# Attention and FFN on one core: pooled scores as four products that share two banks with the local scores, transposes of 96 and 128 columns, and the band mask built for one block and spread by VectorE

## The chip, the core and the metric

The kernel runs on one core of a Trainium2 chip. A core has TensorE (PE: matrix products; a product consists of a weight load, PEld, and a pass of the other operand), VectorE (DVE), ScalarE (ACT), GpSimd (POOL) and SyncE (SP, which here only issues DMAs). They run their own instruction streams in order and wait for each other by semaphores. Products are written to PSUM banks of 128 partitions by 512 float32 values; everything else works on SBUF tiles.

The metric is the device time of one execution in microseconds. The time before is the median of three runs, 1004.47 us (1001.52 to 1006.77).

## The reference

Two attentions are added and put through a feed-forward network. The sizes are: batch 8, 8 heads, 576 positions, 64 values a head; 4608 tokens of 512 values, 2048 hidden values.

```python
def _attn_ref(q, k, v):
    factor = 4
    ...
    q_d = q.reshape(B, H, Sd, factor, D).mean(axis=3)      # k_d and v_d likewise
    out_d = sm_attn(q_d, k_d, v_d)                          # softmax attention over 144 pooled positions
    out_up = np.repeat(out_d, factor, axis=2)
    mask = np.abs(pos[:, None] - pos[None, :]) < factor     # local: a band of +-3 positions
    scores = np.where(mask, scale * q @ k.T, -1e9)
    ...
    return out_up + out_local

def _moe_ref(x, w_in, w_out):
    h = x @ w_in
    return (h * np.cos(h)) @ w_out
```

The feed-forward weights come as float64.

## The kernel before

**Units.** The attention is cut into 32 units: 8 batches times 4 pairs of heads. In a unit, the 64 values of one head lie on partitions 0 to 63 and those of the other on 64 to 127. A unit has these parts:

- `u_qk`: SyncE loads queries and keys (L570), VectorE or GpSimd sums groups of four positions into `qkd` (L577, or L574 and L576), pooled queries and keys of 144 columns.
- `u_s`, scores and softmax. The local scores are 48 products of 32 x 32 (L643): 12 blocks of 32 columns on each of four partition groups, 384 columns in one bank. The pooled scores are 6 products (L652): three groups of 64 queries (0 to 63, 64 to 127, 80 to 143), each for two heads, with the 64 queries as weights and 144 keys as the moving operand, into a second bank of three groups of 144 columns. Then VectorE takes maxima and subtracts (`mxl`, `sml`, `mxd`), ScalarE the exponentials (L678, L679, L681), VectorE sums and reciprocals (L684, L686, L688), and VectorE or GpSimd scales (L690).
- `u_t`: VectorE transposes the local probabilities `sml` (L705). TensorE transposes the pooled ones, `smd`, in two halves of 72 keys: `t_mm` makes two transposes of 128 columns (L714) and a product with 2 x 16 columns of the identity (L716), and ScalarE or VectorE copies the bank to `ptd` (L561, L562).
- `u_pv`: values. Pooled products L759, local ones L771, and the sum of both by VectorE (L782); then the result is split into two float16 parts, the feed-forward input.

**Early and late units.** Batches 0 and 1 are "early" (`NEARLY` = 2). There the band mask is put into the bank by a product of the identity `ident_b` with the mask (L637) before the local products are added, so VectorE reads masked scores straight from the bank (L666, L667). In batches 2 to 7, "late", VectorE adds the mask while it reads the bank (L670). Early score banks come from four named banks, a pair for one unit and the other pair for the next; late ones from a ring of three.

**Feed-forward.** `gemm1` (L811) makes 12 products of 384 columns for each of 16 hidden chunks and 12 token tiles; ScalarE and VectorE make h cos h of it (L825 to L831, L387); `gemm2` (L850) has 9 products of 512 columns. The float64 weights are loaded as integers (L410) and split by VectorE and ScalarE (`w_split`, L422 to L463).

**The order.** Every piece is an operation in a planner with an estimated duration. The planner lists operations by priority, gives those with alternatives to one of two engines (sums of queries and keys, copies from PSUM, scaling), and the program is emitted in the order of planned starts. So a changed estimate can change the order everywhere. Where TensorE has a planned gap in the first 300 us, products of `ident_b` with itself fill it (L988); the first 16 stand at the start of the program. SyncE's loads of the first two batches and the weights are in a fixed order: queries and keys of batch 0, values of batch 0, pooled values of batch 1 (L597, into a ring of 7 buffers, `wd`), weights of chunks 0 and 1, queries and keys of batch 1, and the rest of the weights. A pooled-value buffer comes free when the addition over its four rows is done (`v_add`, L605 and L606, on GpSimd or VectorE).

**Constants.** GpSimd makes two identities, sets the float32 mask of 128 x 384 to zero and cuts the band into it with eight selections of 32 x 384 (L351, L353), sets four corners (L356, L357) and casts it (`mask_b`, L358).

Of the kernel before, what the change touches and what calls it, by code (L numbers as in the profile page):

```python
# [24 lines left out]
P = 128  # L25
# [18 lines left out]
PAD = 3  # L44
SP_ = S + 8
NBLK = 2 * NSEG
QG = 64
NQG = -(-SD // QG)
# [7 lines left out]
NWD = 7  # L56
EARLY = {0: dict(s="pa.0 pa.1 po.0 po.1", t="pa.2", v="ph.0 ph.1"),
# [256 lines left out]
def attn_ffn_kernel(ctx: ExitStack, tc: tile.TileContext, qT, kT, vdn, vl, w_in, w_out, out):  # L314
# [24 lines left out]
    mask, mask_b = const.tile([P, NBLK, BS], F32, name="mask"), const.tile([P, NBLK, BS], BF16, name="mask_b")  # L339

    def constants():
        make_identity(nc, ident_b)
        make_identity(nc, ident)
        dve.memset(bquart, -0.25)
        dve.memset(bhalf, -0.5 * PI)
        dve.memset(ones, 1.0)
        dve.memset(tiny, TINY)
        pool.memset(mask, 0.0)
        for i in range(4):
            h = mask[i * BS:(i + 1) * BS]  # L350
            pool.affine_select(out=h, in_=h, compare_op=ALU.is_ge, fill=NEG, base=0,  # L351
                               pattern=[[0, NBLK], [1, BS]], channel_multiplier=-1)
            pool.affine_select(out=h, in_=h, compare_op=ALU.is_ge, fill=NEG, base=2 * PAD,  # L353
                               pattern=[[0, NBLK], [-1, BS]], channel_multiplier=1)
        for h in range(2):
            pool.memset(mask[2 * BS * h:2 * BS * h + BS, 0, 0:PAD], NEG)  # L356
            pool.memset(mask[2 * BS * h + BS:2 * BS * h + 2 * BS, NBLK - 1, BQ + PAD:BS], NEG)  # L357
        pool.tensor_copy(mask_b, mask)  # L358
# [19 lines left out]
    loads = {}  # L378

    def dma(nbytes, fn, r=(), w=(), pw=()):  # L380
        o = pl.op("SP", max(0.45, nbytes / 262e3), fn, r=r, w=w, pw=pw, lat=1.8)
        loads.setdefault((pl.name,) + pl.arg, []).append(o)
        return o
# [238 lines left out]
    def u_s(b, pr):  # L622
        pl.name = "u_s"
        u = st[(b, pr)]
        q, k, qkd, qkg = u["q"], u["k"], u["qkd"], u["qkg"]
        early = b < NEARLY
        sml, smd = ub(b, pr, "sml"), ub(b, pr, "smd")
        bl, bp = bank(b, "s"), bank(b, "s")
        loc, poo = pl.buf(None), pl.buf(None)

        def using(bk, o):
            bk.r.append(o)
            bk.acc.append(o)

        def l_mm():
            if early:
                pe.matmul(bl.get()[:, :NBLK * BS], ident_b, mask_b.rearrange("p s n -> p (s n)"), start=True, stop=False)  # L637
            for a in range(NSEG // 2):
                for i in range(4):
# [386 lines left out]
```

## Time and profile before

| | us |
|---|---|
| three runs | 1006.77, 1004.47, 1001.52 |
| the profiled execution | 1000.71 |
| its span, first to last instruction | 998.9 |
| TensorE busy | 956.5 |
| VectorE busy | 649.1 |
| ScalarE busy | 601.2 |
| GpSimd busy | 220.2 |

The mean granted clock of TensorE was 0.981 of full speed. The rest of the 1000.71 us lies around the span. In the profile, a group's busy time counts the overlap of neighbours on one engine once; the mean is that of one instruction from its start to its end, and neighbours on TensorE and VectorE overlap. The page's 40 slices of the span, in tenths busy, and the granted clock:

```profile
PE   7788889989999999999999999999999999999998
DVE  5968979697878856745555764755555764544443
PEclk8979979999999999999999999999999999999999
```

A slice is 25 us. TensorE is below nine tenths in the first six slices and the eighth, and VectorE is fullest in the first eleven or so. The small products of the units are a small share: the pooled scores, transposes and local products together stand behind the two feed-forward groups L811 and L850, which carry 33% of the chain each.

### The profile page before, as it was taken

Reading aid. Unit: us, or ns where it says so; the run is one execution under the profiler, and the core shown is the slowest. Engines: PE = TensorE matmul, PEld = TensorE weight load, DVE = VectorE, ACT = ScalarE, POOL = GpSimd, SP = SyncE. Lnnn points to the kernel's source line nnn. Section 1 sums busy time; section 2 is a strip of 40 time slices with the busy share of each in tenths; the row PEclk is TensorE's granted clock in tenths of the full one; section 3 lists DMA queues with packets and bytes.
Section 4 is the critical chain, followed back from the end, with each engine's and each line's share of the span. In section 5 each row is a group of like instructions: output and inputs, shape, how many; then the busy total and the mean of one; then the engine's idle time right before and its main releaser. Section 6 shows DMA issues by size and latency. Waiting matters only on the chain.

```text
span 998.9 us, 26495 instructions
## 1 busy us (share of the span) xinstructions
PE 956.5 (96%) x11333; PEld 558.1 (56%) x11333; DVE 649.1 (65%) x1272; ACT 601.2 (60%) x1225; POOL 220.2 (22%) x360
## 2 busy tenths in 40 slices
PE   7788889989999999999999999999999999999998
PEld 5566445545556655655555665655555665555554
DVE  5968979697878856745555764755555764544443
ACT  2736667677887655656465764656555764644543
POOL 4544823241443311301011320401010210000000
PEclk8979979999999999999999999999999999999999
DMA  8632896576645631321100530321010000000000
GB/s 243 242 124 86 231 270 166 111 168 186 151 85 109 149 78 41 81 57 42 46 27 25 129 90 9 91 63 41 34 41 25 19 34 1 2 32 1 32 1 32
DMA packets 41854, 84.81 MB, mean 85 GB/s; under 512 B 4040, under 2 KB 14536, under 8 KB 41736
## 3 DMA queue, kind: packets, MB, share of 16 engines
q1 hardware_dynamic: 35256, 69.15, 21.6%
q0 software_dynamic: 6480, 13.96, 9.5%
q8 instruction: 89, 1.46, 0.6%
q14 instruction: 29, 0.24, 0.1%
HBM read 65.01 MB, written 18.09 MB: 83 GB/s over the span
## 4 chain that ended last, share of the span: by engine, by line
PE 81%; DVE 6%; ACT 3%; issue 3%; DMA 3%; POOL 2%; POOLq 0%; ACTq 0%; DVEq 0%
PE bank L850 33%; PE bank L811 33%; PE bank L771 4%; PE bank L643 3%; PE bank L652 3%; PE bank L759 2%; PE bank L988 1%; PE bank L714 1%; DMA out<-ob 1%; DMA wd<-vdn 1%; DVE wv L427 1%; DVE tr L826 1%; DVE wv L429 1%; DMA wd<-w_in 1%; ACT wd L435 1%
## 5 line engine op out<-in xcount | busy, mean ns | idle before, releaser
L850 PE MATMUL bank<-wo,gh 128*128 128x512 f16 x1152 | 343.9, 380 | 8.6 <-ACT ob L867 7.3
L811 PEld LDWEIGHTS <-wi 128*128 128x128 f16 x2304 | 225.5, 99 | 178.6 <-issue 12.8
L850 PE MATMUL bank<-wo,gl 128*128 128x512 f16 x576 | 218.6, 380 | 1.4 <-POOL gl L387 1.1
L825 ACT ACTIVATE tr<-bank,bquart,hs 128x384 int32<-128x384 f32 x192 | 128.3, 669 | 108.5 <-PE bank L811 102.8
L826 DVE SCALAR_TENSOR_TENSOR tr<-bank,hs,tr 128x384 f32<-128x384 f32 x192 | 117.9, 615 | 115.3 <-ACT tr L825 114.9
L850 PEld LDWEIGHTS <-gh 128*128 128x128 f16 x1152 | 109.5, 99 | 117.8 <-issue 15.4
L829 DVE SCALAR_TENSOR_TENSOR tr<-tr,rho,bank 128x384 f32<-128x384 f32 x192 | 116.8, 609 | 83.1 <-ACT tr L828 82.8
L828 ACT ACTIVATE tr<-tr,bhalf 128x384 f32<-128x384 f32 x192 | 117.4, 613 | 79.5 <-DVE tr L826 78.5
L831 ACT ACTIVATE gh<-tr 128x384 f16<-128x384 f32 x181 | 94.4, 521 | 113.5 <-DVE tr L829 113.2
L387 DVE TENSOR_TENSOR gl<-tr,gh 128x384 f16<-128x384 f32 x170 | 95.6, 563 | 67.5 <-ACT gh L831 66.2
L811 PE MATMUL bank<-x0h,wi 128*128 128x384 f16 x384 | 103.6, 332 | 7.4 <-DVE tr L829 5.2
L811 PE MATMUL bank<-x1h,wi 128*128 128x384 f16 x384 | 102.9, 330 | 0.0
L811 PE MATMUL bank<-x2h,wi 128*128 128x384 f16 x384 | 101.5, 326 | 0.7 <-DVE tr L829 0.7
L811 PE MATMUL bank<-x3h,wi 128*128 128x384 f16 x384 | 101.5, 326 | 0.0
L850 PEld LDWEIGHTS <-gl 128*128 128x128 f16 x576 | 56.5, 98 | 70.7 <-POOL gl L387 1.6
L574 POOL TENSOR_TENSOR qkd<-q 128x144 f32<-128x144 f32 x25 | 14.6, 585 | 264.6 <-PE bank L652 260.8
L811 PE MATMUL bank<-x0l,wi 128*128 128x384 f16 x192 | 63.8, 332 | 0.0
L811 PE MATMUL bank<-x1l,wi 128*128 128x384 f16 x192 | 63.4, 330 | 0.0
L811 PE MATMUL bank<-x3l,wi 128*128 128x384 f16 x192 | 62.6, 326 | 0.0
L811 PE MATMUL bank<-x2l,wi 128*128 128x384 f16 x192 | 62.6, 326 | 0.0
L771 PE MATMUL bank<-sml,vl 32*64 32x24 f32 x3072 | 53.0, 214 | 1.2 <-issue 0.7
L771 PEld LDWEIGHTS bank<-sml,vl 32*64 32x64 f32 x3072 | 49.4, 135 | 8.0 <-issue 5.2
(155 smaller groups left out, 1208.7 us busy)
## 6 DMA issues: line engine op xcount, KB each, us to landing
vl<-vl SPq DMA_DIRECT2D x32, 384.0 KB, 3.5
q<-qT SPq DMA_DIRECT2D x32, 292.0 KB, 3.7
k<-kT SPq DMA_DIRECT2D x32, 292.0 KB, 4.0
out<-ob SPq DMA_DIRECT2D x36, 256.0 KB, 2.7
out<-ob POOLq DMA_DIRECT2D x33, 256.0 KB, 5.8
wd<-w_in SPq DMA_DIRECT2D x16, 512.0 KB, 4.5
wd<-w_out SPq DMA_DIRECT2D x16, 512.0 KB, 6.3
wd<-vdn SPq DMA_DIRECT2D x18, 384.0 KB, 4.4
```

Source lines behind the costliest of these rows:

```text
L387: f = lambda e: lambda: e.tensor_tensor(out=out(), in0=in0(), in1=in1(), op=ALU.subtract)
L643: pe.matmul(bl.get()[BS * w:BS * (w + 1), BS * c:BS * (c + 1)], q.get()[hs, o:o + BS], k.get()[hs, o:o + BS], start=not early, stop=not ea ...
L652: pe.matmul(bp.get()[hs, g * SD:(g + 1) * SD], qkg()[hs, 0, o:o + QG], qkg()[hs, 1, :], start=True, stop=True)
L759: pe.matmul(banks[0].get()[64 * h:64 * h + 64, 2 * SD:3 * SD], vdg()[:, kh, 64 * h:64 * h + 64], ptd.get()[:, kh, h, :], start=(kh == 0), ...
L771: pe.matmul(banks[e].get()[64 * h:64 * h + 64, o:o + BQ], vt.get()[r, a, i, :], sml.get()[r, 4 * a + i, :BQ], start=True, stop=True)
L811: pe.matmul(ph.get()[:, :m], w[:, i, kc, :], x[:, kc, :], start=(n == 0), stop=(n == 3 * KC - 1))
L825: pl.op("ACT", _act(m, True, 2), lambda: act.activation(ti(), h(), AF.Identity, bias=bquart, scale=inv()), r=[ph, hs], w=[tr])
L826: pl.op("DVE", _dvs(m), lambda: dve.scalar_tensor_tensor(out=tr.get(), in0=h(), scalar=inv(), in1=ti(), op0=ALU.mult, op1=ALU.subtract), r ...
L828: pl.op("ACT", _act(m, False, 1), lambda: act.activation(tr.get(), tr.get(), AF.Sin, scale=2.0 * PI, bias=bhalf), w=[tr], tab="sin")
L829: pl.op("DVE", _dvs(m), lambda: dve.scalar_tensor_tensor(out=tr.get(), in0=tr.get(), scalar=rho(), in1=h(), op0=ALU.mult, op1=ALU.mult), r ...
L831: pl.op("ACT", _act(m, False), lambda: act.activation(gh.get(), tr.get(), AF.Copy), r=[tr], w=[gh], alts=[("DVE", _dve(m / 2), lambda: dve ...
L850: pe.matmul(o, (gh, gh, gl)[k].get()[:, sl], wo.get()[:, (0, 1, 0)[k]], start=(c == c0 and k == 0), stop=(c == c1 - 1 and k == 2))
```

## The change

Five things change.

- **Pooled scores (`d_mm`).** Four products take the place of six. Two have 128 queries (0 to 127) as weights, one for each head (L661 in the changed file); two have 64 queries (80 to 143), one for each head (L664). `HQ` = 48: the last 48 queries are used from these.
- **Banks.** Local and pooled scores are laid over the same two banks. `lcut`: local blocks 0 to 7 lie in bank 0, columns 0 to 255, and blocks 8 to 11 in bank 1 behind the pooled groups. `gcut`: pooled groups 0 (head 0) and 1 (the narrow products) lie in bank 1, group 2 (head 1) in bank 0 behind the local blocks. VectorE's instructions that read scores are split by bank: 8 and 4 blocks, 2 and 1 groups. The mask product of early units is split into 256 and 128 columns. The exponentials of a unit count as readers of both banks.
- **Transposes (`t_mm`).** Two of 96 columns (one for each head) and one of 128 columns, for each half of the keys.
- **Constants.** The band is cut into 128 x 32 first (eight selections of 32 x 32), then GpSimd makes the identities; VectorE casts the band to all 12 blocks (`mask`, now bfloat16) and sets the corners. Late units add the bfloat16 mask.
- **Planner.** The estimates of the changed operations are new numbers, and SyncE's loads get a dependency on a load further back than `AHEAD` = 2^40 bytes.

```diff
-QG = 64
-NQG = -(-SD // QG)
+QG, HQ = 64, 48
+NQG = 3
...
+AHEAD = 1 << 40
...
+        pool.memset(band, 0.0)
+        for i in range(4):
+            h = band[i * BS:(i + 1) * BS]
+            pool.affine_select(out=h, in_=h, compare_op=ALU.is_ge, fill=NEG, base=0, pattern=[[1, BS]], channel_multiplier=-1)
...
         make_identity(nc, ident_b)
+        dve.tensor_copy(mask, band.unsqueeze(1).broadcast_to([P, NBLK, BS]))
...
-        bl, bp = bank(b, "s"), bank(b, "s")
+        banks = [bank(b, "s"), bank(b, "s")]
...
+        lcut, gcut = ((0, 0, 8), (1, 2 * SD, NBLK)), ((1, 0, 2), (0, 8 * BS, NQG))
...
         def d_mm():
-            for g in range(NQG):
-                for h in range(2):
-                    hs, o = slice(64 * h, 64 * h + 64), min(g * QG, SD - QG)
-                    pe.matmul(bp.get()[hs, g * SD:(g + 1) * SD], qkg()[hs, 0, o:o + QG], qkg()[hs, 1, :],
-                              start=True, stop=True)
+            to = [t() for _, _, _, t in cuts(gcut, SD)]
+            for h in range(2):
+                hs = slice(64 * h, 64 * h + 64)
+                pe.matmul(to[h][:, 0], qkg()[hs, 0, :P], qkg()[hs, 1, :], start=True, stop=True)
+            for h in range(2):
+                hs = slice(64 * h, 64 * h + 64)
+                pe.matmul(to[0][hs, 1], qkg()[hs, 0, SD - QG:], qkg()[hs, 1, :], start=True, stop=True)
...
-            using(bl, pl.op("DVE", _dve(n), lambda: dve.tensor_tensor(out=sml.get(), in0=lq(), in1=mask, op=ALU.add), r=[loc], w=[sml]))
+                using(k, "DVE", _dve(w), lambda c=c, src=src: dve.tensor_tensor(out=sml.get()[:, c], in0=src(), in1=mask[:, c], op=ALU.add),
+                      r=[loc], pw=[sml])
...
+        for k, c, w, src in cuts(gcut, SD):
+            using(k, "DVE", _dve(w), lambda c=c, src=src: dve.tensor_reduce(out=mxd.get()[:, c], in_=src(), axis=AX.X, op=ALU.max, negate=True),
+                  r=[poo], pw=[mxd])
...
-                for g in range(NQG - 1):
-                    pe.transpose(to[:, :, g * QG:(g + 1) * QG], smd.get()[:, g, ks], ident)
-                w = SD - (NQG - 1) * QG
-                pe.matmul(to[:, :, SD - w:], smd.get()[:, NQG - 1, ks], ident.rearrange("p (h n) -> p h n", h=2)[:, :, QG - w:],
-                          start=True, stop=True)
+                for h in range(2):
+                    pe.transpose(to[:, h, :SD - HQ], smd.get()[:SD - HQ, 2 * h, ks], ident[:SD - HQ, :SD - HQ])
+                pe.transpose(to[:, :, SD - QG:], smd.get()[:, 1, ks], ident)
```

**TensorE, late units.** The rows from one unit's transposes to another's scores, in a late batch; feed-forward rows that stand between are left out. A row gives line, operation, result and operands, shape and count. Before:

```order
L714 MATMUL bank<-ident,smd 72x2x64 x2
L716 MATMUL bank<-ident,smd 72x2x16
L643 MATMUL bank<-k,q 32x32 x48
L652 MATMUL bank<-qkd 64x144 x6
L850 LDWEIGHTS gh
```

After:

```order
L733 MATMUL bank<-ident,smd 72x96 x2
L734 MATMUL bank<-ident,smd 72x2x64
L652 MATMUL bank<-k,q 32x32 x48
L661 MATMUL bank<-qkd 128x144 x2
L664 MATMUL bank<-qkd 64x144 x2
```

Six pooled products became two wide and two narrow ones, in the same place behind the local products; the narrow product of the identity (L716) became a whole transpose, and the two transposes before it have fewer columns.

**VectorE, the first unit's scores.** From the sums of the first two units (`qkd`) to the first unit's pooled maximum, and what follows. Before:

```order
L577 TENSOR_REDUCE qkd<-k 128x144
L666 TENSOR_REDUCE mxl<-bank 128x12
L577 TENSOR_REDUCE qkd<-q 128x144
L667 TENSOR_TENSOR sml<-bank,mxl 128x384
L673 TENSOR_REDUCE mxd<-bank 128x3
```

After:

```order
L577 TENSOR_REDUCE qkd<-k 128x144
L677 TENSOR_REDUCE mxl<-bank 128x8
L677 TENSOR_REDUCE mxl<-bank 128x4
L679 TENSOR_TENSOR sml<-bank,mxl 128x256
L679 TENSOR_TENSOR sml<-bank,mxl 128x128
L688 TENSOR_REDUCE mxd<-bank 128x2
L688 TENSOR_REDUCE mxd<-bank 128x1
L577 TENSOR_REDUCE qkd<-k 128x144
L577 TENSOR_REDUCE qkd<-q 128x144
```

Three instructions became six, and the sum of the next unit's queries moved behind them. Behind unit 1's pooled maximum (L688) there now stands the addition of pooled values `wd` (L605, L606), which was 19 rows further on. In the changed program the first maximum waits for the wide and narrow pooled products as well, since they write the same banks, and the mask product of units 2 and 3 waits for the exponentials of units 0 and 1.

**GpSimd, the start.** From the sums of queries and keys to the scaling of the first local probabilities (L690 before, L709 after). Before:

```order
L574 TENSOR_TENSOR qkd<-k 128x144
L576 TENSOR_TENSOR qkd<-qkd,k 128x144 x2
L690 TENSOR_TENSOR sml<-sml,su 128x384
L605 TENSOR_TENSOR wd<-wd 72x512
L606 TENSOR_TENSOR vd<-wd 72x256
```

After:

```order
L576 TENSOR_TENSOR qkd<-qkd,k 128x144 x2
L605 TENSOR_TENSOR wd<-wd 72x512
L606 TENSOR_TENSOR vd<-wd 72x256
L605 TENSOR_TENSOR wd<-wd 72x512
L606 TENSOR_TENSOR vd<-wd 72x256
L605 TENSOR_TENSOR wd<-wd 72x512
L606 TENSOR_TENSOR vd<-wd 72x256
L709 TENSOR_TENSOR sml<-sml,su 128x384
```

Three additions of pooled values moved ahead of the scaling.

More of the change, by code (lines that the diff above doesn't have):

```diff
@@ L635, in l_mm, with using, cuts @@
+        def using(k, *a, **kw):
+            o = pl.op(*a, **kw)
+            banks[k].r.append(o)
+            banks[k].acc.append(o)
+        def cuts(cut, size):
+            c = 0
+            for k, at, end in cut:
+                yield k, slice(c, end), (end - c) * size, lambda k=k, at=at, n=end - c: banks[k].get()[:, at:at + n * size].rearrange(
+                    "p (c n) -> p c n", n=size)
+                c = end
         def l_mm():
-            if early:
-                pe.matmul(bl.get()[:, :NBLK * BS], ident_b, mask_b.rearrange("p s n -> p (s n)"), start=True, stop=False)
@@ L638, in l_mm @@
[L638 to L639 removed]
+            for k, c, n, to in cuts(lcut, BS):
+                if early:
+                    pe.matmul(to(), ident_b, mask[:, c], start=True, stop=False)
+                for j in range(c.start, c.stop):
                     for e in range(2):
                         for h in range(2):
[L642 to L644 removed]
+                            hs, o, w = slice(64 * h, 64 * h + 64), (8 * (j // 4) + 4 * e + j % 4) * BQ, 2 * h + e
+                            pe.matmul(to()[BS * w:BS * (w + 1), j - c.start], q.get()[hs, o:o + BS], k_.get()[hs, o:o + BS],
+                                      start=not early, stop=not early or j == c.stop - 1)
@@ L679, in exps @@
             act.activation(sml.get(), sml.get(), AF.Exp, scale=0.125)
-            for g in range(NQG):
-                act.activation(smd.get()[:, g], dq()[:, g], AF.Exp, bias=mxd.get()[:, g:g + 1], scale=1.0 / 128.0,
-                               accum_out=sud()[:, g:g + 1])
-        using(bp, pl.op("ACT", _act(n, False) + 1.2, exps, r=[poo], w=[mxd, sml, smd], pw=[su, part], tab="exp"))
+            for _, c, _, src in cuts(gcut, SD):
+                for g in range(c.start, c.stop):
+                    act.activation(smd.get()[:, g], src()[:, g - c.start], AF.Exp, bias=mxd.get()[:, g:g + 1], scale=1.0 / 128.0,
+                                   accum_out=sud()[:, g:g + 1])
+        o = pl.op("ACT", _act(n, False) + 1.2, exps, r=[poo], w=[mxd, sml, smd], pw=[su, part], tab="exp")
+        for bk in banks:
+            bk.r.append(o)
+            bk.acc.append(o)
         pl.op("DVE", _dve(n), lambda: dve.tensor_reduce(out=sul(), in_=sml.get(), axis=AX.X, op=ALU.add), r=[sml], pw=[su, part])
@@ L975, in spare @@
         return best
-    last = CFG["f0"]
+    last, under = CFG["f0"], []
+    sync = mybir.DependencyInfo(mybir.DependencyClass.Sync, mybir.DependencyReason.SCHED_ONLY)
     with tc.manual_schedule():
@@ L989, in attn_ffn_kernel @@
                 last = o.start + o.dur
-            o.fn()
+            made = o.fn()
+            if size.get(o):
+                room = AHEAD
+                for prior, n in reversed(under):
+                    room -= n
+                    if room < 0:
+                        tc.add_manual_dep(made.ins, prior.name, sync, reason="bytes under way")
+                        break
+                under.append((made.ins, size[o]))
 def _lay(inputs):
```

58 lines of the change are left out of this document (23 added, 35 removed).

## The prediction

> **What bounds the kernel now.** I read the page first (busy shares and chain), then the windows, to see where TensorE has no rest, and then the timeline of one late unit and of the start. The page:
>
> ```profile
> span 998.9 us, 26495 instructions
> PE 956.5 (96%) x11333; PEld 558.1 (56%) x11333; DVE 649.1 (65%) x1272; ACT 601.2 (60%) x1225; POOL 220.2 (22%) x360
> PE 81%; DVE 6%; ACT 3%; issue 3%; DMA 3%; POOL 2%; POOLq 0%; ACTq 0%; DVEq 0%
> ```
>
> TensorE is busy for 96% of the span and carries 81% of the chain. The windows (busy time of PE, PEld, DVE, ACT and POOL in each stretch, then the granted clock and the DMA share) say where that holds:
>
> ```profile
> 0.00:25.00 25.00, 18.15 (x476) 12.58 (x477) 13.66 (x27) 5.51 (x19) 11.35 (x29) 0.86 0.84 242
> 25.00:50.00 25.00, 19.10 (x453) 14.67 (x456) 24.73 (x54) 19.00 (x54) 12.77 (x12) 0.93 0.68 242
> 50.00:75.00 25.00, 21.22 (x577) 15.47 (x576) 16.23 (x42) 9.11 (x35) 10.11 (x20) 0.80 0.37 124
> 300.00:500.00 200.00, 200.00 (x2821) 119.16 (x2813) 130.86 (x257) 119.07 (x238) 42.49 (x65) 1.00 0.32 76
> 500.00:750.00 250.00, 250.00 (x3000) 145.06 (x2998) 148.27 (x283) 148.32 (x292) 42.19 (x63) 1.00 0.20 54
> ```
>
> There are two stages. From 300 to 750 us TensorE is busy for every microsecond at full clock, and VectorE for 59 to 65% of it: only less work on TensorE shortens this part, and VectorE has room. Before that, between 25 and 50 us, VectorE has 24.73 of 25 us, and TensorE has holes. So the change is priced by TensorE's rows in the late units, and by VectorE and the order of things in the first two batches. The windowed list from 220 us on says how many late units there are:
>
> ```profile
> L652 PE MATMUL bank<-qkd 64*64 64x144 f32 x288 | 22.9, 291 | 0.0
> L714 PE MATMUL bank<-ident,smd 128*72 128x128 f32 x96 | 17.1, 274 | 0.0
> ```
>
> 288 rows at 12 a unit is 24 units, all six late batches, with no idle time ahead of them: what a late unit saves on TensorE is saved on the end.
>
> **Pooled scores in a late unit.** One late unit in the timeline (start, duration, line, count; a group's duration runs on beyond the next start, so I take start to start):
>
> ```profile
> 299.84 1.02 PE L643 MATMUL bank<-k,q 64*32 64x32 f32 x96
> 300.79 0.95 PE L652 MATMUL bank<-qkd 64*64 64x144 f32 x12
> 301.67 0.11 PEld L850 LDWEIGHTS <-gh 128*128 128x128 f16 x2 [0.20 <-issue]
> ```
>
> Six products run as 12 passes, those of the two row halves side by side, so six rounds, in 301.67 − 300.79 = 0.88 us. Four products make 8 passes, four rounds if the two heads still run side by side. Against that stand the change of the tile's shape between the wide (64x128) and the narrow (64x64) products, and weight loads of 128 columns in place of 64. The nearest rows for four rounds and for a change of shape are those of the value products:
>
> ```profile
> 304.38 0.71 PE L759 MATMUL bank<-ptd,vsum 72*64 72x144 f32 x8
> 305.02 1.59 PE L771 MATMUL bank<-sml,vl 32*64 32x24 f32 x96
> 306.54 0.61 PE L850 MATMUL bank<-wo,gh 128*128 128x512 f16 x2
> ```
>
> L759 makes four rounds (8 passes) in 305.02 − 304.38 = 0.64 us, with a change of shape, to L771, at its end. So two rounds more cost 0.88 − 0.64 = 0.24, or 0.12 a round, and four bare rounds would be 0.48: start and end with their changes of shape hold the other 0.16. My four products have one change more, in the middle, which costs between 0 and 0.16; I take 0.1, nearer to the row: 0.64 + 0.1 = 0.74. Wider weights may add 0.02 to each of the two wide rounds (the quoted 128-column load of L850 takes 0.11 us, which a round of 0.12 nearly covers): **0.78 us, saving 0.10**. Bounds: 0.64 (the change hidden) saves 0.24; 0.98 (six rounds and a change, when the wide heads don't run side by side) loses 0.10. Side by side is likely, since the wide products of the two heads write two banks, and L771 already has row groups that write the same partitions of two banks: its 96 passes take 306.54 − 305.02 = 1.52 us, 16 ns each, far under a round. Times 24: **−2.4 us** (−5.8 to +2.4).
>
> The Trainium skill, in "TensorEngine Tiling (Array Packing)", section Key Properties, says that changing the tiling mode, not just the tile, drains TensorE. By that rule the four products pay for two drains, as in my sum, where six paid for one; without it the pooled part would be 0.64 and the six batches would gain 5.8 us. The 0.16 us around L759's rounds agree with it, though they don't split into a drain and the rest.
>
> **Transposes.** Two of them stand together in this unit:
>
> ```profile
> 311.09 0.38 PE L714 MATMUL bank<-ident,smd 128*72 128x128 f32 x2
> 311.31 0.26 PE L716 MATMUL bank<-ident,smd 128*72 128x32 f32 x2
> 311.40 0.60 PE L850 MATMUL bank<-wo,gh 128*128 128x512 f16 x2
> ```
>
> Two transposes of 128 columns take 311.31 − 311.09 = 0.22, 0.11 each; the rest product of L716 takes 0.09, though it has few columns. After: two transposes of 96 columns (0.11 × 96/128 = 0.082 each) and one of 128 (0.11), 0.27 in place of 0.31: −0.04, for 48 of them **−1.9 us**. Bounds: 0.33 if a 96-column transpose costs a whole one (+0.02, so +1.0), 0.25 if the last one overlaps with what follows (−2.9).
>
> **Extra VectorE work.** Masking and the pooled maximum are split by bank. The groups:
>
> ```profile
> L673 DVE TENSOR_REDUCE mxd<-bank 128x3 f32<-128x432 f32 x32 | 19.3, 603 | 8.2 <-PE bank L652 7.5
> L666 DVE TENSOR_REDUCE mxl<-bank 128x12 f32<-128x384 f32 x8 | 4.4, 554 | 6.7 <-PE bank L643 6.7
> L670 DVE TENSOR_TENSOR sml<-bank,mask 128x384 f32<-128x384 f32 x24 | 13.2, 551 | 1.3 <-PE bank L643 1.2
> ```
>
> 603 ns for 432 elements and 554 for 384 is 1.0 ns an element and 0.16 us for being an instruction at all, of which back-to-back starts hide about half: 0.07 to 0.16 us for each extra one. Late units get two extra, 24 × 2 × 0.16 = 8 us at most, under TensorE at 59 to 65% of VectorE: nothing, unless a unit's transposes come late by it; without that cover it would be up to +8. Early units get three extra each, 8 × 3 = 24, or 1.7 to 3.8 us, and there VectorE is full: **+2 us**. The constants that move to VectorE (a cast and four small settings) fall before 3.7 us, when it waits for the first load.
>
> **The first 20 us.** Rows of TensorE, GpSimd, VectorE and ScalarE there:
>
> ```profile
> 1.01 0.29 POOL masks.py:199 TENSOR_SCALAR_AFFINE_SELECT ident_b<-ident_b 128x128 bf16<-128x128 bf16 x1
> 1.36 3.59 PE L988 MATMUL bank<-ident_b 128*128 128x256 bf16 x16 [1.36 <-POOL ident_b masks.py:199]
> L351 POOL TENSOR_SCALAR_AFFINE_SELECT mask<-mask 32x384 f32<-32x384 f32 x4 | 2.3, 578 | 0.2
> 8.46 0.32 PE L637 MATMUL bank<-mask_b,ident_b 128*128 128x384 bf16 x1 [3.51 <-POOL vq L471]
> 10.20 0.56 DVE L666 TENSOR_REDUCE mxl<-bank 128x12 f32<-128x384 f32 x1 [2.06 <-PE bank L643]
> 10.61 1.70 PE L652 MATMUL bank<-qkd 64*64 64x144 f32 x12
> 13.01 0.20 ACT L678 ACTIVATE mxd<-mxd 128x3 f32<-128x3 f32 x1 [10.99 <-DVE mxd L673]
> 14.51 0.20 ACT L681 ACTIVATION_READ_ACCUMULATOR smd<-bank,mxd 128x1 f32 x1
> 18.79 1.14 PE L643 MATMUL bank<-k,q 64*32 64x32 f32 x96
> 20.18 0.20 ACT L681 ACTIVATION_READ_ACCUMULATOR smd<-bank,mxd 128x1 f32 x1
> 20.35 1.02 PE L643 MATMUL bank<-k,q 64*32 64x32 f32 x96
> ```
>
> TensorE waits 3.51 us for the mask. Eight selections of 0.58 us become eight of a twelfth of the size, but they now stand ahead of `ident_b`. A select of 128 columns takes 0.29 and a setting of little more than nothing 0.1; between these I take 0.2, so `ident_b` is ready 8 × 0.2 + 0.2 = 1.8 us later, the 16 fillers run from 3.2 to 6.8, and the first mask product comes at 6.8 where it came at 8.46: 1.7 us earlier (bounds 0.9 to 2.6). That is not kept. Local and pooled scores now share both banks, and in the changed program VectorE's first maximum waits for the pooled products, not for the last local one. Before, it began at 10.20, under the pooled products; now it begins at their end, 12.3 − 1.7 = 10.6, and two maxima, two subtractions (0.55 × 2 + 0.2) and two pooled maxima (0.7) make 2.0 us before ScalarE starts at 12.7, against 13.01: **−0.3**. Behind the waiting maximum stand VectorE's sums of queries and keys for the next units, which TensorE needs only after the second unit. The other new wait is that units 2 and 3 can't begin their masks until the exponentials of units 0 and 1 are read out of the shared banks. Those ended at 14.7 and 20.4, and the local scores of units 2 and 3 began at 18.79 and 20.35: the first has room, the second becomes a wait of about nothing.
>
> **Loads.** SyncE's longest wait and the loads it ended with, and VectorE's longest wait in the second batch:
>
> ```profile
> SPq L597 <- DVE su L684: 14.7, 1, 14.7
> 13.78 17.80 SPq L597 DMA_DIRECT2D wd<-vdn  x3
> 64.19 0.61 DVE L673 TENSOR_REDUCE mxd<-bank 128x3 f32<-128x432 f32 x1 [3.65 <-PE bank L652]
> ```
>
> A load of value rows waited 14.7 us for a buffer that VectorE had to clear, till 13.78 + 17.80 = 31.6 us, and all weights and the second batch stood behind it in SyncE's queue. The addition that clears it now comes ahead of the scaling of the local probabilities on GpSimd, and straight after unit 1's pooled maximum on VectorE, which precedes the exponentials that ended at 20.4; so the queue goes on some 10 us earlier. Loads that come early help only where VectorE idles for them: it idles 8.8 us of 50 to 75, of which 3.65 in the row above. I take 2.5 of that as gained (bounds 0 and 8.8): **−2.5**.
>
> **Sum.** −2.4 − 1.9 + 2.0 − 0.3 − 2.5 = −5.1 us. The profiled execution took 1000.71 us (a span of 998.9 and 1.8 around it), so such a run would take 995.6. It is 3.8 below the median of the three runs, 1004.47 (1001.52 to 1006.77); on that median the forecast is **999.4**. 0.5% is 5.0 us, about what a measurement of this kernel can tell from no change.
>
> **The rivals.**
> No steady gain: the wide heads run one after the other, or the drains and weight loads eat the two rounds. For it: weights of twice the columns, and two changes of shape. Against it: L771's row groups. The pooled part loses 2.4, the transposes gain 1.9, the early terms give −0.8: 1004.2.
> Slower, by the banks: in each early batch the second pair of units waits on exponentials of the first, and VectorE has nothing else in that time. Price: the exponentials, 14.7 − 13.01 = 1.7, and the next scores, 0.95 + 0.88, make 3.5 us a wait, one in each of two batches 7.0, with the 2.0 of extra instructions 9.0, less 4.3 of the steady gain, and nothing from start and loads: +4.7, 1009.2. It decides when VectorE has less than 3.5 us of other work queued there. For it: idle VectorE in 0 to 25 us (11.3 of 25). Against it: 24.73 busy of 25 to 50.
> Earlier loads count for more: the holes of 50 to 75 us close nearly whole (8.8), the first GEMM comes that much earlier, and the rest stands: 1004.47 − 2.4 − 1.9 + 2.0 − 0.3 − 8.8 = 993.1.
> The limit on bytes under way that the diff also adds does nothing: its room is 2^40 bytes, and the page counts 84.81 MB moved in all.
>
> **How the numbers follow.** Forecast 0.46, no steady gain 0.17, slower 0.16, more by loads 0.21. The forecast's own bounds put a bit over half of it beyond −5.0. Faster by over 0.5%: 0.26 + 0.21 = 0.47; within: 0.20 + 0.16 + 0.05 = 0.41; slower: 0.11 + 0.01 = 0.12. The range takes in the third rival nearly whole, and the slower one up to 1008: 991 to 1008, with about 0.2 outside.
>
> **What would show it.** Pooled products from first to next line 0.78 (0.64 would mean no drain, 0.98 one head after the other); transposes 0.27; the first mask product at 6.8 us; the first exponential at 12.7; TensorE still full from 300 us. I am wrong if a late unit's TensorE rows don't shrink, or if the end of the early part (the first stretch with TensorE full, 225 us here) moves by over 5 us either way; the order between 75 and 220 us is shuffled by the change, and I priced that at nothing.

## The result and the profile after

Fourteen runs of each kernel side by side: 1009.56 us before (median, 1001.52 to 1014.67) and 998.72 us after (997.21 to 1000.98). The ratio is 0.9901, with a 95% interval from 0.9878 to 0.9924: the change makes the kernel about 10.8 us faster, twice the 5.1 us that were forecast. Here and below, a ratio is taken between runs of one session, without executions in a visibly slower state, so it need not be the quotient of the two medians. The time itself, 998.7, is near the forecast 999.4 only because the three runs shown before lay low: a median of 1004.47, against 1009.56 of fourteen.

The two profiles hide most of it, and this is the first thing to see. The changed kernel's execution took 999.18 us, its span 997.4; that of before 1000.71 and 998.9. They are 1.5 us apart, since the profiled execution of before is faster than any of the fourteen timed ones. The page after, as before (span, busy times, chain by engine):

```profile
span 997.4 us, 26159 instructions
PE 961.3 (96%) x11133; PEld 554.9 (56%) x11133; DVE 663.2 (66%) x1362; ACT 601.4 (60%) x1229; POOL 208.9 (21%) x334
PE 77%; DVE 8%; ACT 5%; issue 4%; DMA 3%; POOL 2%; SPq 0%; POOLq 0%; ACTq 0%; DVEq 0%
```

VectorE has 14 us more work, TensorE is busy 5 us longer, and still the kernel is faster. A product at half clock is also busy for longer (the same two products of `gemm2` take 0.59 us at full and 1.01 at half clock, in rows of before further down), so TensorE's busy time says little of the work here. The rows of a late unit, line numbers of the changed file (L652 local, L661 wide and L664 narrow pooled products, L733 and L734 transposes, L828 and L867 the feed-forward):

```profile
307.90 0.33 PE L733 MATMUL bank<-ident,smd 96*72 96x96 f32 x2
308.07 0.27 PE L734 MATMUL bank<-ident,smd 128*72 128x128 f32 x1
308.18 0.59 PE L867 MATMUL bank<-wo,gh 128*128 128x512 f16 x2
...
310.52 0.52 PE L661 MATMUL bank<-qkd 64*128 64x144 f32 x4
310.96 0.46 PE L664 MATMUL bank<-qkd 64*64 64x144 f32 x4
311.36 0.34 PE L828 MATMUL bank<-x2h,wi 128*128 128x384 f16 x1
```

Pooled scores: 311.36 − 310.52 = 0.84 us, 0.88 before. Transposes: 308.18 − 307.90 = 0.28, 0.31 before. Over 24 units that is 24 x 0.04 + 48 x 0.03 = 2.4 us.

To place the rest I mark the start of ScalarE's first step on each of the 192 feed-forward chunks (L825 before, L842 after: `tr<-bank,bquart,hs`), counted from 0. The stage from chunk 0 to chunk 24 is the one in which TensorE still has holes (before, the ninth slice of 25 us, 200 to 225 us, is still below nine tenths); the columns are length, busy time of PE, PEld, DVE, ACT and POOL, granted clock, DMA share. Before, and after:

```profile
89.17:216.59 127.42, 111.45 (x598) 59.55 (x596) 106.59 (x212) 87.99 (x174) 55.56 (x96) 0.95 0.74 194
```

```profile
103.35:219.72 116.37, 104.40 (x579) 56.98 (x579) 105.96 (x215) 94.80 (x191) 59.06 (x102) 0.99 0.79 217
```

In the changed kernel chunk 0 comes 14.2 us **later**. Then the stage to chunk 24 takes 116.4 us where it took 127.4, with the same 106 us of work on VectorE (91% of the stage, 84% before), and from chunk 24 to the end it takes 777.7 where it took 782.3. So three parts have to be explained: a late start, a shorter stage, and 4.6 us less behind it.

The shorter stage is not all density. TensorE idles for 12.0 us of it where it idled for 16.0, its clock is higher (0.99 against 0.95), and it holds fewer products: 289 of `gemm1` and 207 of `gemm2` in place of 300 and 216. At the 0.162 and 0.216 us from start to start that these take at full clock, I estimate that 3.7 of the 11 us are products that now run outside this stage. Ahead of chunk 0, TensorE has the products of the same eight early units in both, so the time from chunk 0 to the end compares the same rest of the work: 894.1 us where it was 909.8, 15.7 less in these two executions.

### The profile page after: what moved, and what is told of

It is laid out like the page before. It is cut to its first block, busy times and chain, and to the rows that moved or that the text cites. A ratio compares the mean times of both kernels' runs of the same rounds, so it can differ in the third digit from the quotient of the medians.

```text
span 997.4 us, 26159 instructions
## 1 busy us (share of the span) xinstructions
PE 961.3 (96%) x11133; PEld 554.9 (56%) x11133; DVE 663.2 (66%) x1362; ACT 601.4 (60%) x1229; POOL 208.9 (21%) x334
## 4 chain that ended last, share of the span: by engine, by line
PE 77%; DVE 8%; ACT 5%; issue 4%; DMA 3%; POOL 2%; SPq 0%; POOLq 0%; ACTq 0%; DVEq 0%
PE bank L828 30%; PE bank L867 30%; PE bank L788 5%; PE bank L652 3%; PE bank L1006 2%; PE bank L776 2%; DMA wd<-vdn 2%; PE bank L661 2%; PE bank L664 1%; DVE tr L846 1%; PE bank L733 1%; DMA k<-kT 1%; DVE wv L427 1%; DVE tr L843 1%; DVE wv L429 1%
## 5 line engine op out<-in xcount | busy, mean ns | idle before, releaser
L867 PE MATMUL bank<-wo,gh 128*128 128x512 f16 x1152 | 343.0, 379 | 3.7 <-ACT ob L884 3.5
L828 PEld LDWEIGHTS <-wi 128*128 128x128 f16 x2304 | 224.4, 98 | 169.6 <-issue 8.9
L867 PE MATMUL bank<-wo,gl 128*128 128x512 f16 x576 | 218.4, 379 | 0.1
L842 ACT ACTIVATE tr<-bank,bquart,hs 128x384 int32<-128x384 f32 x192 | 128.2, 668 | 118.5 <-PE bank L828 115.2
L867 PEld LDWEIGHTS <-gh 128*128 128x128 f16 x1152 | 110.8, 98 | 114.1 <-issue 8.4
L846 DVE SCALAR_TENSOR_TENSOR tr<-tr,rho,bank 128x384 f32<-128x384 f32 x192 | 116.8, 609 | 78.6 <-ACT tr L845 78.4
L848 ACT ACTIVATE gh<-tr 128x384 f16<-128x384 f32 x173 | 90.1, 521 | 81.1 <-DVE tr L846 79.6
L828 PE MATMUL bank<-x0h,wi 128*128 128x384 f16 x384 | 102.4, 329 | 2.3 <-DVE tr L846 1.7
L828 PE MATMUL bank<-x2h,wi 128*128 128x384 f16 x384 | 101.5, 326 | 1.0 <-DVE tr L846 1.0
L828 PE MATMUL bank<-x1h,wi 128*128 128x384 f16 x384 | 102.2, 328 | 0.0
L828 PE MATMUL bank<-x3h,wi 128*128 128x384 f16 x384 | 101.5, 326 | 0.0
L867 PEld LDWEIGHTS <-gl 128*128 128x128 f16 x576 | 56.3, 98 | 68.7 <-DVE gl L387 0.6
L709 POOL TENSOR_TENSOR sml<-sml,su 128x384 f32<-128x384 f32 x25 | 28.3, 1132 | 166.5 <-DVE su L707 161.7
L828 PE MATMUL bank<-x0l,wi 128*128 128x384 f16 x192 | 63.1, 329 | 0.0
L828 PE MATMUL bank<-x1l,wi 128*128 128x384 f16 x192 | 63.0, 328 | 0.0
L828 PE MATMUL bank<-x3l,wi 128*128 128x384 f16 x192 | 62.6, 326 | 0.0
L828 PE MATMUL bank<-x2l,wi 128*128 128x384 f16 x192 | 62.6, 326 | 0.0
L788 PE MATMUL bank<-sml,vl 32*64 32x24 f32 x3072 | 56.1, 220 | 2.0 <-issue 1.8
L788 PEld LDWEIGHTS bank<-sml,vl 32*64 32x64 f32 x3072 | 52.6, 144 | 9.4 <-issue 7.7
```

The costliest lines, as they stand in the source:

```text
L709: f = lambda e, sm=sm, f=f, bc=bc: lambda: e.tensor_tensor(out=sm.get(), in0=sm.get(), in1=wide(f(), bc), op=ALU.mult)
L788: pe.matmul(banks[e].get()[64 * h:64 * h + 64, o:o + BQ], vt.get()[r, a, i, :], sml.get()[r, 4 * a + i, :BQ], start=True, stop=True)
L828: pe.matmul(ph.get()[:, :m], w[:, i, kc, :], x[:, kc, :], start=(n == 0), stop=(n == 3 * KC - 1))
L842: pl.op("ACT", _act(m, True, 2), lambda: act.activation(ti(), h(), AF.Identity, bias=bquart, scale=inv()), r=[ph, hs], w=[tr])
L846: pl.op("DVE", _dvs(m), lambda: dve.scalar_tensor_tensor(out=tr.get(), in0=tr.get(), scalar=rho(), in1=h(), op0=ALU.mult, op1=ALU.mult), r ...
L848: pl.op("ACT", _act(m, False), lambda: act.activation(gh.get(), tr.get(), AF.Copy), r=[tr], w=[gh], alts=[("DVE", _dve(m / 2), lambda: dve ...
```

## The experiments

Each theory's numbers stood before its run. The stage from chunk 0 to 24, and the rest, were read from the profile of each. The runs of before in the same session have a median of 1008.0 us for e1 to e4, 1006.0 for e5 to e8 and 1008.1 for e9 to e12.

**e1: before once more.** No edit.

> The kernel of before unchanged, for a second profile of it. Its 14 runs spread from 1001.5 to 1014.7 us and the one that was profiled (1000.7) is the fastest; the 14 runs of the changed kernel spread from 997.2 to 1001.0. Theory A (the start varies): a profile near the median, 1005 to 1014, has the same time from its 48th feed-forward chunk to the end as the first profile, within 1 us, and the 5 to 13 us more lie before that chunk. Theory B (everything is a little slower, clock or memory): the excess grows evenly over the span, about half of it behind the 96th of 192 chunks. Ratio to before 1.00 under both.

Ratio 0.9991 (0.9953 to 1.0028), runs from 992.8 to 1013.2. Its profile was an even faster execution (span 991.1), which answers the question as well: chunk 0 comes 4.3 us earlier than in the first profile, chunk 32 comes 8.2 us earlier, and from chunk 48 on every chunk is 7.86 to 7.88 us earlier up to the last. So theory A: an execution is decided before chunk 48, and one profile of before can lie anywhere within some 20 us.

**e2: two numbers of the planner.**

```diff
-            pl.op("PE", 1.52, l_mm, r=[vt, sml], pw=banks, w=loc)
+            pl.op("PE", 1.55, l_mm, r=[vt, sml], pw=banks, w=loc)
...
-            pl.op("PE", 2.16, lambda: (d_mm(), l_mm()), r=[vd, ptd, vt, sml], pw=banks, w=loc + [poo])
+            pl.op("PE", 2.22, lambda: (d_mm(), l_mm()), r=[vd, ptd, vt, sml], pw=banks, w=loc + [poo])
```

> The kernel of before with two numbers of the planner alone (the estimates of the value products, 1.52 to 1.55 and 2.16 to 2.22): no operation is changed, only the order that the planner makes. Theory 1 (the gain is less work on TensorE and the earlier start): within 3 us of before. Theory 2 (the gain of 10 us is mostly another order of the first 220 us): over 4 us away from before in either direction, and chunks 0 to 16 of the feed-forward move by several us.

Ratio 0.9988 (0.9944 to 1.0033): no change. Another order is not always another time. Chunk 0 stood 16 us later in its profile, but after e1 that can be the execution and not the order.

**e3: the new constants alone,** on the kernel before.

```diff
-        make_identity(nc, ident_b)
-        make_identity(nc, ident)
...
-        pool.tensor_copy(mask_b, mask)
+        pool.memset(band, 0.0)
...
+        make_identity(nc, ident_b)
+        dve.tensor_copy(mask, band.unsqueeze(1).broadcast_to([P, NBLK, BS]))
```

> Before with the new constants alone (band for one block, spread by VectorE, identities later, bfloat16 mask for late units); the planner's order is the same. Theory 1: the first mask product at about 7.0 us instead of 8.46, the first exponential 1.5 us earlier, and 0 to 2 us less at the end. Rival: the start is not on the path (loads and stalls of the instruction stream set the first batch), 0 within 1 us. Neither expects the 10 us.

Ratio 0.9953 (0.9922 to 0.9984), some 5 us: more than either theory had, but see e6. Its profile (span 1007.7, near before's usual time) is of use for the start: chunk 0 at 101.4, and the stage to chunk 24 takes 123.8.

**e4: pooled products and shared banks alone.** `u_s` of the changed file, transposes and constants of before; the transposes then read the pooled probabilities in the old layout, so the pooled output is permuted.

> Before with the pooled scores as four products, the shared banks and the split VectorE instructions, with their planner estimates; transposes and constants as before (so the transposes read the pooled probabilities in the old layout, and the pooled output is permuted). Theory 1: 24 x 0.04 = 1.0 us less on TensorE in the late units (0.84 in place of 0.88), and with the banks' waits at the start -3 to +4 at the end. Theory 2: the order that comes with it matters more: 5 to 12 us faster or slower.

Ratio 0.9997 (0.9971 to 1.0024): nothing. Stage 125.6, rest 781.9. SyncE's first weight load goes at 27.1 us (31.7 in the first profile of before).

**e5: all four products wide.** Head 1's second one goes over its own first result, so group 1 of head 1 is missing.

```diff
-                pe.matmul(to[0][hs, 1], qkg()[hs, 0, SD - QG:], qkg()[hs, 1, :], start=True, stop=True)
+                pe.matmul(to[h][:, 1 - h], qkg()[hs, 0, SD - P:], qkg()[hs, 1, :], start=True, stop=True)
```

> The changed kernel with the two narrow pooled products made wide too (128 queries; head 1's goes over its own first result), so the four products have one shape; the order is the same. In the late units the changed kernel has 0.23 from the first wide round to the second, 0.22 to the first narrow, 0.17 to the second narrow and 0.21 to the next line: 0.84. If changing the shape in the middle costs a drain and a second uncovered weight load: 0.23 + 0.13 + 0.13 + 0.21 = 0.70. If a round of wide products is slow by itself: 0.23 + 0.2 + 0.2 + 0.21 = 0.84, no gain.

Its one run took 993.87 us. One late unit of its timeline:

```profile
308.26 0.52 PE L661 MATMUL bank<-qkd 64*128 64x144 f32 x4
308.61 0.41 PE L664 MATMUL bank<-qkd 64*128 64x144 f32 x4
308.95 0.34 PE L828 MATMUL bank<-x2h,wi 128*128 128x384 f16 x1
```

308.95 − 308.26 = 0.69 where the changed kernel has 0.84: mixing the two shapes costs 0.15 us a unit. From chunk 24 to the end it takes 774.4 us against 777.7: 3.3 = 24 x 0.14. The first theory holds. This way of counting from chunk 24 on is good to about 1 us: the two profiles of before, and those of the changed kernel and of e8, differ by 1.4 and 0.9 there.

**e6: the old constants in the changed kernel,** the order unchanged (the edit of e3 the other way round).

> The changed kernel with the constants of before, the planner's order unchanged. If the earlier mask product is worth something: +1 to +3 us over the changed kernel's 998.7 (its first mask product at 8.5 again). If the start hides behind instruction arrival and loads: 0 within 1. If the wide spread of before belongs to its constants (TensorE starting at 1.4 and stopping at 5 us): the runs spread over 10 us as before's do.

997.66 us, ratio 0.9868 (0.9781 to 0.9955), four runs from 989.3 to 1001.3: not slower, so in this order no gain of the constants shows, as far as four runs with this spread can tell. e3's 5 us are not found again here, and it stays open whether they belong to the old order or to chance. Its runs spread over 12 us, where the changed kernel's spread over 4; but e3's, with the new constants, spread over 18, so the constants by themselves don't set the spread.

**e7: the old transposes in the changed kernel.** They read the new layout, so the pooled output is permuted. The expectation says that the order is unchanged; it was not, since the estimate 0.26 came back with the old code.

```diff
-                for h in range(2):
-                    pe.transpose(to[:, h, :SD - HQ], smd.get()[:SD - HQ, 2 * h, ks], ident[:SD - HQ, :SD - HQ])
-                pe.transpose(to[:, :, SD - QG:], smd.get()[:, 1, ks], ident)
-            pl.op("PE", 0.29, t_mm, r=[smd], w=[bk])
+                for g in range(NQG - 1):
+                    pe.transpose(to[:, :, g * QG:(g + 1) * QG], smd.get()[:, g, ks], ident)
...
+            pl.op("PE", 4 * 0.065, t_mm, r=[smd], w=[bk])
```

> The changed kernel with before's transposes (two of 128 columns and the 16-column product; the pooled probabilities are then read in another layout, which permutes the pooled output), planner's order unchanged. Work theory: 48 x 0.03 = +1.5 us, all of it behind chunk 24. Order theory expects the same here, and that nothing before chunk 24 moves.

1013.55 us, ratio 1.0057 (1.0024 to 1.0091): 15 us over the changed kernel, and slower than before. In the profiles, 13.7 of 14.9 us stand ahead of chunk 48. This miss opened the question that e9 and e10 take apart: the transposes, or the order.

**e8: twice the fillers** between 8 and 110 us.

```diff
-                for _ in range(max(n, CFG["warm"][o.arg[0]] if early and s else 0)):
+                for _ in range((1 if o.start < 8 or o.start > 110 else 2) * max(n, CFG["warm"][o.arg[0]] if early and s else 0)):
```

> The changed kernel with each group of fillers between 8 and 110 us twice as long (136 more products of 0.1 to 0.2 us). Clock theory: TensorE's half-speed stretches (15 to 20, 25 to 41, 55 to 69, 83 to 102 us in the changed kernel's profile) each follow an idle gap of 1.7 to 4 us; where fillers close such a gap the stretch goes, and the first feed-forward chunk comes 3 to 10 us earlier than 103. Rival: the gaps are instruction arrival or waits that fillers can't fill, and the fillers only delay products: 0 to 10 us later.

995.99 us (four runs), ratio 0.9882 (0.9814 to 0.9950), chunk 0 at 96.7 instead of 103.4, granted clock 0.983 to 0.990. The fifty microseconds from 50 to 100 us show what differs. The changed kernel, then e8, then e10 (below):

```profile
50.00:100.00 50.00, 43.58 (x1026) 31.98 (x1024) 36.72 (x100) 23.27 (x73) 13.59 (x21) 0.68 0.32 110
```

```profile
50.00:100.00 50.00, 46.26 (x1164) 34.59 (x1158) 42.62 (x114) 24.84 (x77) 15.52 (x23) 0.93 0.33 115
```

```profile
50.00:100.00 50.00, 45.31 (x1086) 33.02 (x1082) 45.46 (x121) 28.26 (x81) 17.75 (x27) 0.84 0.35 116
```

The clock that TensorE is granted is 0.68 in the mean, 0.93 with more fillers, and with it VectorE gets through more instructions in the same time (114 and 121 against 100). I read this as the small products of the first batches holding up VectorE's work when they run at half clock; no run shows that step by itself. Where the half-speed stretch of the changed kernel begins:

```profile
77.80 1.35 PE L788 MATMUL bank<-sml,vl 32*64 32x24 f32 x77
80.98 0.53 PE L788 MATMUL bank<-sml,vl 32*64 32x24 f32 x19 [1.84 <-issue]
```

```profile
80.00:90.00 10.00, 8.96 (x159) 6.83 (x163) 5.40 (x14) 2.28 (x7) 1.70 (x2) 0.60 0.01 4
90.00:100.00 10.00, 9.94 (x216) 8.01 (x212) 5.76 (x12) 4.00 (x11) 0.00 (x0) 0.50 0.16 43
```

TensorE stops for 1.84 us in the middle of a group of products, for which the profile shows no releaser, and then runs at half clock until about 102 us. In the fourteen profiles together, chunk 0 comes at 84.9 to 97.0 us where TensorE was granted half clock for 10 to 31 us ahead of it, and at 99.3 to 105.6 where for 44 to 58; only e12 (31 us, 103.9) falls out.

**e9: one number.** The changed kernel, all its operations, with the order of e7.

```diff
-            pl.op("PE", 0.29, t_mm, r=[smd], w=[bk])
+            pl.op("PE", 4 * 0.065, t_mm, r=[smd], w=[bk])
```

> The changed kernel with one number of the planner as before (the estimate of the transposes 0.26 in place of 0.29), every operation as in the changed kernel: only the order differs, and it is the order of e7. Order theory: e7's 1013.6 was the order, so this comes at 1009 to 1014, some 1.5 us under e7. Work theory (e7's 15 us came from its transposes): 998 to 1000, as the changed kernel.

1005.01 us, ratio 0.9989 (0.9949 to 1.0030): most or all of the gain is gone, with every operation of the change in place. It came lower than the 1009 to 1014 expected; its profiled execution (1009.6 span) is a long one. The loss is not in the start: chunk 0 comes 3.3 us earlier than in the changed kernel, and from there to the end it takes 15.5 us longer. The stage of e9, to be held against the two rows of the result:

```profile
100.04:226.58 126.54, 111.77 (x609) 61.70 (x609) 106.87 (x221) 94.38 (x190) 55.97 (x102) 0.95 0.76 209
```

Again 107 us of work on VectorE, and 126.5 us for it.

**e10: the old transposes in the changed kernel's order** (e7 with the estimate at 0.29; the output is permuted as there).

> The changed kernel with before's transposes at the estimate 0.29, so every engine's order is the changed kernel's. Work theory with the rows' size: 48 x 0.03 = 1.5 us behind chunk 24, 1000 in all. If the transposes were worth 15 us: 1013.

988.07 us (987.85 to 988.56), ratio 0.9806 (0.9758 to 0.9855): both expectations fail, it is 10.6 us *under* the changed kernel. Behind chunk 24 it is 1.2 us slower (778.8 against 777.7), as the size of the rows wants it. But its clock holds better in the start (0.84 above), chunk 0 comes 14 us earlier, at 89.3, which is more than these 10.6 us, and its stage is nearly as short as the changed kernel's:

```profile
89.30:207.95 118.65, 106.14 (x580) 57.64 (x580) 107.92 (x219) 94.65 (x193) 60.09 (x103) 0.97 0.78 220
```

e7 and e10 also have the same operations and differ in that one number: 1013.55 and 988.07 us, ratios 1.0057 and 0.9806. So with either kind of transposes the changed kernel's order is the faster one, by 6 to 9 us with the new ones and by 25 with the old ones.

**e11: all six numbers of the planner on the kernel before,** no operation changed.

> Before with all six changed estimates of the planner and no changed operation. Order theory: another order, so another time, 4 us or more from before's 1006 to 1008 in either direction; if it is this order that the change owes its gain to, 1000 to 1004. Work theory: within 3 us of before.

Ratio 1.0021 (0.9982 to 1.0060): no change; stage 127.7. The order that pays is not made by the new numbers alone; the new operations, which the planner also sees (more of VectorE's instructions, other banks and waits), have a part in it.

**e12: e8 once more.**

> e8 once more with more runs. Clock theory: granted clock 0.983 to 0.990 against 0.965 to 0.974 for the changed kernel, and 2 to 5 us under its 998.7. Rival (e8's four runs were luck): 998 to 1000.

994.95 us (six runs, 990.8 to 1003.0), ratio 0.9878 (0.9829 to 0.9927), clock 0.980 to 0.991. By the medians of e8 and e12 this is the fastest of these kernels that computes everything, 2 to 4 us under the changed one by ratios and medians; the intervals overlap, so that gain is not shown. The profiled execution, the slowest of the six, has chunk 0 at 103.9 us, no earlier than the changed kernel, though its clock ahead of chunk 0 is 0.85 against 0.72.

All profiles together, in us:

| kernel | chunk 0 at | 0 to 24 | 24 to end |
|---|---|---|---|
| changed | 103.4 | 116.4 | 777.7 |
| e5 all wide | 99.3 | 118.3 | 774.4 |
| e6 old constants | 105.6 | 116.3 | 777.6 |
| e8 more fillers | 96.7 | 117.2 | 778.6 |
| e10 old transposes, same order | 89.3 | 118.6 | 778.8 |
| e12 more fillers again | 103.9 | 119.5 | 777.8 |
| before | 89.2 | 127.4 | 782.3 |
| e1 before again | 84.9 | 125.2 | 780.9 |
| e3 constants | 101.4 | 123.8 | 782.4 |
| e2 two numbers | 105.6 | 123.7 | 778.0 |
| e4 pooled | 97.0 | 125.6 | 781.9 |
| e7 | 100.1 | 125.5 | 786.6 |
| e9 one number | 100.0 | 126.5 | 783.0 |
| e11 all numbers | 89.4 | 127.7 | 783.6 |

The six profiles with the changed kernel's order need 116 to 120 us for the stage, whatever their transposes, constants, pooled products or fillers; the eight others, of five orders, need 124 to 128. From chunk 0 to the end the six need 893 to 897 us and the eight 902 to 912. The clock is not what separates them, though it has a part: at 0.97 in the stage, as in e10, e4 needs 125.6 us,

```profile
97.00:222.57 125.57, 109.19 (x608) 60.50 (x607) 104.97 (x214) 90.63 (x182) 58.08 (x100) 0.97 0.75 204
```

and e2 needs 123.7 at the 0.99 of the changed kernel. This time behind chunk 0 is where the larger part of the gain lies.

## Why the prediction was right, and where it was not

**The direction, the range and the sign of the steady terms were right**; the sum −5.1 was half of the measured −10.8, and its terms were not the ones that carried it.

*Pooled scores, −2.4 forecast, −1.0 measured.* The step was "0.64 + 0.1 = 0.74. Wider weights may add 0.02 to each of the two wide rounds". The change of shape is as I had it: from the second wide round to the first narrow one takes 0.22 us, and a round among equals 0.12, so 0.10 more. What I undersized is the round after a new shape: 0.23 from the first wide to the second, 0.17 from the first narrow to the second, where I had 0.14 and 0.12. e5 measures both costs of the mixture together, 0.15. The rival of no steady gain is out; the heads do run side by side. A cost such as the drain named from the Trainium skill ("TensorEngine Tiling (Array Packing)", Key Properties) is there: without the second shape the four products take 0.69. How much of it is a drain, and how much a weight load that nothing covers, e5 does not tell.

*Transposes, −1.9 forecast, −1.2 to −1.4 measured* (e10 behind chunk 24; 48 x 0.03 by the rows). The 96-column transposes come 0.085 apart, as scaled, but the last one takes 0.11 to the next line, where the 16-column product it replaces took 0.09 with two passes: so 0.28 instead of 0.27.

*VectorE's extra work, +2.0 in the early units.* The split instructions have the size forecast. The two pooled maxima:

```profile
L688 DVE TENSOR_REDUCE mxd<-bank 128x2 f32<-128x288 f32 x32 | 14.3, 447 | 0.0
L688 DVE TENSOR_REDUCE mxd<-bank 128x1 f32<-128x144 f32 x32 | 9.5, 296 | 0.0
```

447 + 296 = 743 ns where one took 603: 0.14 us for each extra one, within 0.07 to 0.16. In the stage from chunk 0 on it changes nothing (the stage holds 106 us of VectorE either way), and what it did to the start can't be told from the clock's swings.

*The first 20 us, −0.3 forecast.* The steps came in the order worked out, and then were lost. The changed kernel:

```profile
6.98 0.27 PE L647 MATMUL bank<-mask,ident_b 128*128 128x256 bf16 x1
...
9.19 0.46 PE L664 MATMUL bank<-qkd 64*64 64x144 f32 x4
9.30 0.69 DVE L677 TENSOR_REDUCE mxl<-bank 128x8 f32<-128x256 f32 x2 [1.41 <-PE bank L661]
...
11.13 0.20 ACT L693 ACTIVATE mxd<-mxd 128x3 f32<-128x3 f32 x1 [9.12 <-DVE mxd L688]
...
15.47 0.26 PE L652 MATMUL bank<-k,q 64*32 64x32 f32 x2 [4.04 <-issue]
...
19.21 0.20 ACT L693 ACTIVATE mxd<-mxd 128x3 f32<-128x3 f32 x1 [6.38 <-DVE mxd L688]
```

The mask product comes at 6.98 (6.8 forecast, 8.46 before), and the first exponentials at 11.1, earlier than the 12.7 forecast: the pooled products ran at full clock and took 0.83 us where I carried over the 1.70 of before, and the first maximum waited for the wide products alone (L661); the narrow ones (L664) still ran when it began, at 9.30. Then TensorE stops for 4.04 us (1.84 in the first profile of before), with no releaser in the profile, and the second unit's exponentials begin at 19.2 instead of 18.7. e6 agrees: in this order no worth of the constants shows.

*Loads, −2.5 forecast.* The queue did go on 10 us earlier:

```profile
11.97 10.03 SPq L597 DMA_DIRECT2D wd<-vdn  x4
22.10 0.47 SPq L410 DMA_DIRECT2D wd<-w_in  x1
```

The blocked loads are done at 22.0 us (31.6 before). But earlier loads alone bring nothing: e4, e9 and e7 have the first weight load at 27.1, 26.3 and 24.7, and keep a stage of 125.5 to 126.5 us and no gain to speak of. Term and rival ("earlier loads count for more") are not borne out as priced; that the dense order also needs them is possible and was not tried apart.

*The order, priced at nothing.* This is the step that failed: "the order between 75 and 220 us is shuffled by the change, and I priced that at nothing". It carries the larger part of the gain. With equal starts, e10 and the first profile of before (chunk 0 at 89.3 and 89.2) have stages that are 8.8 us apart. e9 shows it from the other side: one number, no operation, and most or all of the gain is gone. Since nothing in the sum stood for the order, and none of the five other orders profiled has so short a stage, the sign of this part was luck. In before's stage TensorE waits for copies of its result banks, once even in a row, three groups of one chunk:

```profile
123.88 0.59 PE L850 MATMUL bank<-wo,gh 128*128 128x512 f16 x2 [1.85 <-ACT ob L867]
124.31 0.38 PE L850 MATMUL bank<-wo,gl 128*128 128x512 f16 x1
126.75 1.01 PE L850 MATMUL bank<-wo,gh 128*128 128x512 f16 x2 [2.06 <-ACT ob L867]
127.56 0.63 PE L850 MATMUL bank<-wo,gl 128*128 128x512 f16 x1
129.43 1.01 PE L850 MATMUL bank<-wo,gh 128*128 128x512 f16 x2 [1.24 <-DVE ob L868]
```

5.2 us are lost here, and the products after the second wait run at half clock (1.01 instead of 0.59). It is the largest such place. But it is not what makes every other order slow: waits for these copies come to 8.5 us in before's stage and 3.0 in the changed kernel's, but only 2.4 in e9's, which is as long as before's and waits 6.4 us for L846 on VectorE instead. How the changed kernel's order comes to be the faster one stays open.

*The slower rival* (the banks' waits) is out as priced: units 2 and 3 found their banks free. Their mask products began at 20.0 and 26.1 us, and the exponentials of units 0 and 1 had ended at 12.8 and 20.9. But the start did get slower: chunk 0 comes 14 us later than in the first profile of before, with the clock at 0.68 instead of 0.87 between 50 and 100 us:

```profile
50.00:100.00 50.00, 42.99 (x1043) 31.60 (x1038) 38.46 (x93) 26.49 (x78) 20.32 (x35) 0.87 0.32 105
```

A profile of before at its usual time would have chunk 0 at about 99 (an estimate: 1008 less 1.8 around the span, less the 907 us that e1, e3 and the first profile have from chunk 0 to the end, in the mean). By that estimate, and by the mean of the same three profiles, the change costs some 4 us there, gains 9 in the stage and 4 behind it. Of these 4, the rows' sizes explain 2.4; the rest I put down to the order, which moves this part by as much (e2, with no operation changed, has 778.0 there, e9, with all of them, 783.0).

*The signs.* The rows shrank, and TensorE is full from 300 us. The end of the early part tells nothing: TensorE idles for 0.5 us in each of 225 to 230 and 240 to 245 us, where before has no hole until 270 us, but two executions of before differ by 8 us at chunk 32, more than the 5 us that I allowed.

*The base.* I put the sum against a profiled execution that was 9 us below the kernel's usual time, and took three runs for its spread. Nothing in the page said so; only the distance of 3.8 us to the median hinted at it.

## What to carry to other kernels

Where a planner sets the order, a change of operations is two changes: measure the operations in the old order, and the new order with the old operations. Here the operations' rows are worth 2.4 us, and the order 6 to 9 (the changed kernel against e9, by medians and by ratios). Before pricing a start of 100 us from one execution, profile the same kernel twice: from chunk 48 on two executions agreed to 0.02 us, and ahead of it they differed by 8.

## What the runs showed of the hardware

- TensorE's granted clock falls to 0.50 for 3.4 to 24 us at a time in the first 105 us of these profiles, mostly after a stop of 1.3 to 4.8 us (1.84 us ahead of the stretch from 82 to 102 us in the changed kernel, where TensorE was busy for 9.0 us of 80 to 90 and 9.9 of 90 to 100). Not each stop does it: in the first profile of before TensorE stood still for 2.8 us from 24.9 us on and went on at full clock. With 136 more fillers of 0.1 to 0.2 us the mean clock from 50 to 100 us rose from 0.68 to 0.93 (e8) and 0.90 (e12).
- Stops without a releaser last differently long in two executions of one program: 2.23 us in e8 and 3.59 in e12, in the same group of products, at 11.9 and 12.4 us. Their places are fixed: in all fourteen profiles, each of the 55 such stops of 0.6 us or more in the first 110 us lies at TensorE's 450th instruction, weight loads and products counted, or a multiple of 256 instructions from it, to within one. Instructions that arrive in blocks of 256 would do this; no run tried it.
- Two programs with one order, which differ in their transposes alone, have their own clock in the start, run after run: 0.965 to 0.974 over the whole kernel for the changed one (fourteen runs), 0.981 to 0.984 for e10 (four). Why stays open.
- A change of tile shape between two products costs about 0.10 us, and the first round in the new shape 0.05 to 0.06 more (0.17 and 0.23 against 0.12 and 0.17).
